# First head's queries and keys by a casting DMA, mask rows by DMA, and a fixed load order at the start of a fused attention and mixer kernel

## The chip, the cores and the metric

The kernel runs on one core of one Trainium2 chip. The metric is device time in microseconds: 287.15 us before the change, the median of 6 runs (286.35 to 287.81). A profile of one execution is used beside it. Engines in the profile: PE (TensorE matmul), PEld (TensorE weight load), DVE (VectorE), ACT (ScalarE), POOL (GpSimd) and SP (SyncE, here only a DMA queue). DMAs are also issued from ACT's and POOL's queues.

## The reference

A block-sparse attention is followed by a mixer. For each of 4 batches and 8 heads, 768 positions of 64 numbers:

```python
mask = np.abs(blk_i - blk_j) <= window            # blocks of 32, 24 of them
mask = mask | (blk_i == 0) | (blk_j == 0) | (blk_i == n_blocks - 1) | (blk_j == n_blocks - 1)
for qb in range(n_blocks):                        # and 3 sampled blocks for each
    for kb in sampled_blocks[qb]:
        mask[qb * block:(qb + 1) * block, kb * block:(kb + 1) * block] = True
scores = np.where(mask, scale * q @ k.T, -1e9)
attn = softmax(scores) @ v
...
# x is the attention's output, heads side by side: (4, 768, 512)
u = x + (x.transpose(0, 2, 1) @ U @ V).transpose(0, 2, 1)   # U 768x32, V 32x768
out = u + np.maximum(u @ w_ch1, 0) @ w_ch2                  # 512 -> 2048 -> 512
```

All inputs and the output are float32; the kernel computes in float16 with float32 sums.

## The kernel before

Work goes by pairs of heads, 16 pairs in all, four to a batch. Position p*6 + t of the sequence lies on partition p in slice t, so each head of q, k or v is loaded as 128 rows of 384 numbers. A pair's q and k are loaded in float32 by SP (`load_qk`, L147), cast to float16 by POOL (`cast`, L138) into a staging tile `stqld` or `stkld`, and turned on PE. Values are loaded and cast the same way (`load_v`, L160) into `vt`.

**Masking in the first batch (pairs 0 to 3).** The mask is put into the score's matmul. A head's query tile `qres[i]` has 64 rows of queries and 24 rows that say in one-hot form which block a position is in; the key tile `kres[i]` has 64 rows of keys and 24 rows of bias per block (0 or -240). Head 0 of a pair has its data in partitions 0 to 63 and mask rows from 64 on, head 1 the other way round (`drows`, `mrows`, L127). There are two such sets, used in turn by pairs; `second_set` (L310) fills the mask rows of the second from the first by DMA. The one-hot rows and the fixed part of the mask come from one constant in DRAM, `small_const`. The bias is worked out on DVE from the sampled block ids (`sb`) and that constant (L262 to L269), and PE spreads it over the positions (`mask_half`, L237).

A score (L652) is 128 keys by 768 queries in two matmuls; ACT makes its exponential (L661) into `est`; PE multiplies that with the values (L381). From pair 4 on, a mask tile is multiplied in on DVE instead (L690), made in the first batch from `kmask` (L611). The mixer's matmuls (L552 and L576) are woven in from then on.

**The order.** PE, DVE and ACT follow the program's order inside `manual_schedule` (L221 for the start, L782 for the rest; there SP too). In the rest, the order is written out as a string of words, `PLAN` (L403): `S` is a score, `e` its exponential, `A` a value product, `R` and `t` the turn of the next pair's q or k on PE and its copies on DVE (L624), `Z` and `z` the same for the first pair's second head (L295), `K` and `k` a part of the mask. It begins `S0 S3 e Z7 e z S0 S5 e Z2 e A7 z S3 A A e S0 S5 e A R2 e S3 t R1 e A A t S5 v e S3 S1`. POOL's instructions, and SP's at the start, are ordered by a planner, in general in the program's order. A DMA of SP or ACT takes one of eight semaphores in turn, and so waits for the DMA eight before it to land.

**The start before.** ACT issues the block ids, SP the constants, then q and k of head 0 and q and k of head 1 (L186), the values of pair 0, q, k and v of pair 1, the one-hot rows of head 1 (L311), and those of the second set. PE does nine warming matmuls (`keep_warm`, L229). DVE sets four tiles to zero (L226), casts head 0's q (L200), and ACT casts its k; PE turns both against the identity (`first_turn`, L204), and ACT and DVE copy the turned halves into `qres[0]` and `kres[0]` (`first_row`, L248). ACT copies head 0's one-hot rows (L255). `mask_row` (L245) copies the bias rows. POOL casts head 1's q and k, and PE turns them as words `Z` of the plan.

Of the kernel before, what the change touches and what calls it, by code (L numbers as in the profile page):

```python
# [21 lines left out]
def kernel(  # L22
# [80 lines left out]
    def psc2():  # L103
        ring["psc"] += 1
        return PS[:, (0, 3)[ring["psc"] % 2] :][:, 0:2]
# [8 lines left out]
    id16 = consts.tile([P, P], FP16)  # L114
# [21 lines left out]
    sts = {}  # L136
# [22 lines left out]

    def load_v(i):  # L160
        b, hp = divmod(i, HP)
        ld = ldpool.tile([P, 2, T, D], FP32, tag="ldv", name="vld")
        nc.sync.dma_start(
            out=ld,
            in_=v[b, 2 * hp : 2 * hp + 2].rearrange("h (p t) d -> p h t d", t=T),
        )
        cast(i, vts[b % 2][:, 2 * hp : 2 * hp + 2, :, 0:D], ld)
# [1 line left out]

    NPAIR = B * HP  # L170
    NPE = HP + 2
    nc.scalar.dma_start(
        out=sb[0:NB].rearrange("k z r w -> k (z r w)"),
        in_=sampled_blocks.bitcast(I32).rearrange("z r -> (z r)")[None, :].broadcast_to(
            [NB, NB * 6]
        ),
    )
    nc.sync.dma_start(out=small[0:NB, :], in_=small_dr.ap())
    nc.sync.dma_start(out=id16, in_=eye_dr.ap())
    lds = {}  # L180
    for h in range(2):
        for src, nm in ((q, "qld"), (k, "kld")):
            if h == 0:
                lds[nm] = ldpool.tile([P, 2, T, D], FP32, tag="ld" + nm, name=nm)
                sts[0, nm] = stpool.tile([P, T, 2, D], FP16, tag="st" + nm, name="st" + nm)
            nc.sync.dma_start(  # L186
                out=lds[nm][:, h], in_=src[0, h].rearrange("(p t) d -> p t d", t=T)
            )


    warm = nc.const_aps.tensor(1.0, [P, 512], mybir.dt.bfloat16)
    bias = consts.tile([P, 2, D], FP16)
    for vt in vts:
        nc.gpsimd.memset(vt[:, :, :, D : D + 1], 1.0)
    for tile_ in (Ut, Vt, kmask):
        nc.gpsimd.memset(tile_, 0.0)

    def first_cast(h, n, copy):
        nm = ("qld", "kld")[n]
        copy(out=sts[0, nm][:, :, h], in_=lds[nm][:, h])  # L200

    first_out = {}

    def first_turn(h, n, c):  # L204

        if n == 1:
            pt = psm([P, HS], FP32)
        elif c == 0:
            pt = pw[:, 1, 0:HS]
        else:  # L210
            pt = psc2()[:, 0, 0:HS]
        first_out[n, c] = pt
        for j in range(3):
            nc.tensor.matmul(
                pt[0:D, j * P : (j + 1) * P],
                sts[0, ("qld", "kld")[n]][:, 3 * c + j, h],
                id16,
                start=(j == 0), stop=(j == 2), skip_group_check=True,
            )

    with tc.manual_schedule(  # L221
        engines={mybir.EngineType.PE, mybir.EngineType.DVE, mybir.EngineType.Activation}
    ):
        nc.vector.memset(bias, 0.0)
        for res in (*qres, *kres):
            nc.vector.memset(res, 0.0)  # L226
        pw = psc2()

        def keep_warm(n, cols=512):  # L229
            for _ in range(n):  # L230
                nc.tensor.matmul(  # L231
                    pw[:, 0, 0:cols], warm[:, 0:P], warm[:, 0:cols], start=True, stop=True
                )

        pks = [bank(6, [P, HS], FP32), psm([P, HS], FP32)]

        def mask_half(c):  # L237
            nc.tensor.matmul(
                pks[c],
                bias[0:NB].rearrange("k a z -> k (a z)"),  # L240
                ohT[:, c * HS : (c + 1) * HS],
                start=True, stop=True,
            )

        def mask_row(h, c, copy):  # L245
            copy(out=kres[0][mrows[h], h, c * HS : (c + 1) * HS], in_=pks[c][mrows[h]])

        def first_row(n, c, copy):  # L248
            copy(
                out=(qres, kres)[n][0][drows[0], 0, c * HS : (c + 1) * HS],  # L250
                in_=first_out[n, c][0:D],
            )

        keep_warm(9)
        nc.scalar.copy(out=qres[0][mrows[0], 0, :], in_=ohT)  # L255
        first_cast(0, 0, nc.vector.tensor_copy)
        first_turn(0, 0, 0)
        first_turn(0, 0, 1)

        eq = consts.tile([P, NB, 3], FP32)  # L260
        a01 = consts.tile([P, NB], FP32)
        nc.vector.tensor_scalar(  # L262
            out=eq[0:NB], in0=sb[0:NB, :, :, 0], scalar1=iota, scalar2=-1.0,
            op0=ALU.is_equal, op1=ALU.add,
        )
        nc.vector.tensor_reduce(
            out=a01[0:NB], in_=eq[0:NB], axis=mybir.AxisListType.X, op=ALU.max
        )
        nc.vector.scalar_tensor_tensor(  # L269
            out=bias[0:NB, :, 0:NB], in0=a01[0:NB, None].broadcast_to([NB, 2, NB]),  # L270
            scalar=-MASK_BIAS, in1=ms[:, None].broadcast_to([NB, 2, NB]),
            op0=ALU.mult, op1=ALU.max,
        )
        first_cast(0, 1, nc.scalar.copy)
        first_turn(0, 1, 0)
        first_row(0, 0, nc.vector.tensor_copy)
        first_row(0, 1, nc.scalar.copy)
        mask_half(0)
        first_row(1, 0, nc.scalar.copy)
        first_turn(0, 1, 1)  # L280
        mask_half(1)
        keep_warm(2, 256)
        mask_row(0, 0, nc.vector.tensor_copy)
        first_row(1, 1, nc.vector.tensor_copy)
        mask_row(0, 1, nc.vector.tensor_copy)
        mask_row(1, 0, nc.vector.tensor_copy)
        mask_row(1, 1, nc.vector.tensor_copy)


    results = {}  # L290
# [4 lines left out]
    def last_turn(n, k_):  # L295
        pt = bank(k_, [P, S], FP16)
        for t in range(T):
            nc.tensor.transpose(
                out=pt[:, t * P : (t + 1) * P],
                in_=sts[0, ("qld", "kld")[n]][:, t].rearrange("p h d -> p (h d)"),  # L300
                identity=id16,
            )
        then(
            "z",
            lambda: nc.vector.tensor_copy(
                out=(qres, kres)[n][0][drows[1], 1, :], in_=pt[drows[1], :]
            ),
        )

    def second_set():  # L310
        nc.sync.dma_start(  # L311
            out=qres[0][mrows[1], 1, :], in_=small_dr.ap()[:, 2 * NB + 2 :]
        )
        for h in range(2):
            nc.sync.dma_start(
                out=qres[1][mrows[h], h, :], in_=small_dr.ap()[:, 2 * NB + 2 :]
            )
            nc.sync.dma_start(out=kres[1][mrows[h], h, :], in_=kres[0][mrows[h], h, :])
        nc.sync.dma_start(out=kmask[mrows[0], :], in_=kres[0][mrows[0], 0, :])

    def load_mix():
        uld = ldpool.tile([P, T, R], FP32, tag="ldu", name="uld", bufs=1)
        nc.sync.dma_start(out=uld, in_=moe_U.rearrange("(p t) r -> p t r", t=T))
        vld = ldpool.tile([P, 2, T, D], FP32, tag="ldv", name="vld")
        vld = vld.rearrange("p h t d -> p (h t d)")
        nc.sync.dma_start(out=vld[0:R, :], in_=moe_V)
        nc.gpsimd.tensor_copy(out=Ut[:, :, 0:R], in_=uld)
        nc.gpsimd.tensor_copy(
            out=Vt[0:R, :, :], in_=vld[0:R, :].rearrange("r (p t) -> r t p", t=T)
        )  # L330

    def load_w1(cs):
# [381 lines left out]

    bts[0] = Batch()
    pairs = {}
    for n in range(2):
        first_cast(1, n, nc.gpsimd.tensor_copy)
    load_v(0)
    load_qk(1)  # L720
    load_v(1)
    second_set()
    load_mix()

    def begin(i):
        if i and i % HP == 0:
            bts[i // HP] = Batch()
# [102 lines left out]
```

## Time and profile before

| what | value |
|---|---|
| median of 6 runs | 287.15 us |
| the profiled execution's own time | 287.17 us |
| its span | 285.4 us |
| PE busy in the span | 277.8 us |
| ACT busy | 179.6 us |
| DVE busy | 198.4 us |
| POOL busy | 69.5 us |

A line of the timeline gives start and length in us, engine, line of the kernel, operation, output <- input, shape and count; in brackets the idle time before it and what ended that. `SPq`, `ACTq` and `POOLq` are DMA issues. A busy PE is not PE at its peak: the ends of matmuls are modelled. The granted clock is 1.00 in every stretch.

### The profile page before, as it was taken

To read this page: it belongs to the slowest core of one execution; us is meant where nothing else is said; L and a number is where in the kernel's file an instruction comes from. 1 tells how busy PE (TensorE), PEld (TensorE's weight loads), DVE (VectorE), ACT (ScalarE), POOL (GpSimd) and SP (SyncE) were. 2 spreads that over 40 slices of the span, in tenths; PEclk is the share of its full clock that TensorE was granted. 3 is DMA by queue.
4 is the path that set the end of the run, shared out by engine and by line. 5 is a ranking of instruction groups with operands and counts; after the bars stand their busy time and mean duration, and the time that the engine had idled before them with its cause. 6 is when DMAs were issued, how large, how long until landed. Compare 5 with 4: busy or idle time off the path is not lost.

```text
span 285.4 us, 6732 instructions
## 1 busy us (share of the span) xinstructions
PE 277.8 (97%) x2771; PEld 163.9 (57%) x2771; DVE 198.4 (70%) x360; ACT 179.6 (63%) x212; POOL 69.5 (24%) x157
## 2 busy tenths in 40 slices
PE   8789999999999999999999999999999999999995
PEld 3557775657456654567556564565745565555553
DVE  7488989998768966788687885666866888231121
ACT  4799998885678566775776627777588730424200
POOL 4566133902242052500451032700310000000000
PEclk9999999999999999999999999999999999999999
DMA  5799979799271479108460398303741103001012
GB/s 155 243 283 289 226 207 214 150 143 226 58 230 39 91 227 253 58 24 222 100 214 2 95 234 203 135 20 59 225 87 39 39 37 87 17 0 40 37 55 92
DMA packets 46430, 36.78 MB, mean 129 GB/s; under 512 B 28000, under 2 KB 42912, under 8 KB 46400
## 3 DMA queue, kind: packets, MB, share of 16 engines
q1 hardware_dynamic: 43532, 32.02, 40.8%
q0 software_dynamic: 2688, 4.19, 8.3%
q8 instruction: 21, 0.34, 0.5%
q10 hardware_dynamic: 180, 0.15, 0.2%
q14 instruction: 9, 0.07, 0.1%
HBM read 27.66 MB, written 6.29 MB: 119 GB/s over the span
## 4 chain that ended last, share of the span: by engine, by line
PE 88%; DVE 8%; DMA 2%; issue 1%; ACT 0%; DVEq 0%
PE ps L552 29%; PE ps L576 28%; PE ps L381 11%; PE ps L675 9%; PE ps L652 3%; DMA qres<-small_const 2%; PE ps L465 2%; PE ps L499 2%; PE ps L231 1%; PE ps L596 1%; DVE xh L446 1%; DVE mask L619 1%; DVE xf L446 1%; PE ps L627 1%; DVE est L690 1%; DVE u L506 1%
## 5 line engine op out<-in xcount | busy, mean ns | idle before, releaser
L684 ACT ACTIVATE est<-ps 128x1536 f16<-128x1536 f32 x72 | 100.4, 1449 | 31.3 <-PE ps L675 31.3
L552 PE MATMUL ps<-uT,w1t 128*128 128x384 f16 x512 | 95.6, 326 | 0.4 <-DVE xf L509 0.2
L576 PE MATMUL ps<-w2t,tT 128*128 128x512 f16 x368 | 88.8, 379 | 0.0
L690 DVE TENSOR_TENSOR est<-est,mask 128x1536 f16<-128x1536 f16 x72 | 69.1, 962 | 13.4 <-ACT est L684 13.2
L564 ACT ACTIVATE tT<-ps 128x384 f16<-128x384 f32 x87 | 42.1, 493 | 54.0 <-PE ps L552 52.4
L552 PEld LDWEIGHTS <-w1t 128*128 128x128 f16 x512 | 47.4, 98 | 36.8 <-issue 6.6
L576 PEld LDWEIGHTS <-tT 128*128 128x128 f16 x368 | 34.4, 98 | 36.5 <-issue 2.9
L381 PEld LDWEIGHTS <-est 128*128 128x128 f16 x1152 | 40.8, 97 | 8.0 <-issue 2.3
L381 PE MATMUL ps<-vt,est 128*128 128x65 f16 x1152 | 43.2, 193 | 1.3 <-POOL vt L141 1.2
L566 DVE TENSOR_SCALAR tT<-ps 128x384 f16<-128x384 f32 x41 | 22.8, 555 | 30.6 <-PE ps L552 30.0
L144 POOL CAST stqld<-qld 128x192 f16<-128x192 f32 x40 | 15.4, 427 | 112.6 <-DMA qld<-in_q_dram 94.9
L661 ACT ACTIVATE est<-ps 128x768 f16<-128x768 f32 x48 | 35.2, 813 | 2.8 <-PE ps L652 2.8
L675 PE MATMUL ps<-qpl,kpl 64*128 64x512 f16 (+1 forms) x288 | 31.3, 325 | 0.0
L652 PE MATMUL ps<-qres,kres 128*128 128x384 f16 x96 | 22.4, 324 | 1.6 <-DVE kres L637 0.6
L584 DVE TENSOR_TENSOR of<-xf,ps 128x512 f32<-128x512 f32 x23 | 15.8, 685 | 9.8 <-PE ps L576 9.6
L675 PEld LDWEIGHTS <-kpl 64*128 64x128 f16 x288 | 11.7, 94 | 15.4 <-issue 9.5
L506 DVE TENSOR_TENSOR u<-xh,ps 128x384 f16<-128x384 f16 x28 | 15.4, 552 | 7.0 <-PE ps L499 6.1
L446 DVE TENSOR_TENSOR xh<-ps,rcp 128x384 f16<-128x384 f32 x32 | 17.8, 557 | 1.1
L446 DVE TENSOR_TENSOR xf<-ps,rcp 128x384 f32<-128x384 f32 x32 | 17.5, 547 | 0.0
L144 POOL CAST vt<-vld 128x192 f16<-128x192 f32 x40 | 15.3, 423 | 3.8 <-DMA vld<-in_v_dram 2.2
L144 POOL CAST stkld<-kld 128x192 f16<-128x192 f32 x40 | 16.0, 440 | 0.7 <-DMA kld<-in_k_dram 0.7
L509 DVE TENSOR_TENSOR xf<-xf,ps 128x384 f32<-128x384 f32 x28 | 15.4, 549 | 0.0
(78 smaller groups left out, 145.7 us busy)
## 6 DMA issues: line engine op xcount, KB each, us to landing
vld<-in_v_dram SPq DMA_DIRECT2D x16, 384.0 KB, 6.3
out_dram<-of SPq DMA_DIRECT2D x23, 256.0 KB, 4.0
qld<-in_q_dram SPq DMA_DIRECT2D x15, 384.0 KB, 4.4
kld<-in_k_dram SPq DMA_DIRECT2D x15, 384.0 KB, 4.7
w1t<-in_moe_w_ch_dram POOLq DMA_DIRECT2D x4, 512.0 KB, 10.5
w2t<-in_moe_w_ch_dram POOLq DMA_DIRECT2D x4, 512.0 KB, 7.4
qld<-in_q_dram SPq DMA_DIRECT2D x2, 192.0 KB
kld<-in_k_dram SPq DMA_DIRECT2D x2, 192.0 KB, 4.8
```

The source lines that it names most:

```text
L144: last = nc.gpsimd.tensor_copy(out=dst[:, h, ts], in_=ld[:, h, ts])
L381: nc.tensor.matmul(pav[:, sc, :], est[:, n, sc * P : (sc + 1) * P], vts[b % 2][:, 2 * hp + h, g, 0 : D + 1], start=(g == 0 and sc == 0), s ...
L446: self.last = nc.vector.tensor_tensor(out=dst, in0=pav[:, :, 0:D], in1=rcp[:, :, None].broadcast_to([P, T, D]), op=ALU.mult,)
L552: nc.tensor.matmul(pt, w1t[:, cc, jj * P : (jj + 1) * P], bts[b].uT[cc][:, c * HS : (c + 1) * HS], start=(cc == 0), stop=(cc == NCC - 1), ...
L564: nc.scalar.activation(out=dst, in_=pt, func=AF.Relu)
L566: nc.vector.tensor_scalar_max(out=dst, in0=pt, scalar1=0.0)
L576: nc.tensor.matmul(po, tts[b, c, jj][:, s * P : (s + 1) * P], w2t[:, jj, :], start=(jj == 0), stop=(jj == NJJ - 1),)
L652: nc.tensor.matmul(ps[:, c], kT[:, h, g * P : (g + 1) * P], qT[:, h, c * HS : (c + 1) * HS], start=True, stop=True,)
L661: lambda: nc.scalar.activation(out=dst, in_=ps, func=AF.Exp, scale=0.125),
L675: nc.tensor.matmul(units[h][:, u * S + lo : u * S + hi], kT[drows[h], g * P : (g + 1) * P], qT[drows[h], lo:hi], start=True, stop=True, sk ...
L684: nc.scalar.activation(out=both[h], in_=units[h].rearrange("p (g n) -> p g n", g=2), func=AF.Exp, scale=0.125,)
L690: lambda: nc.vector.tensor_mul(out=both[h], in0=both[h], in1=mask[:, 2 * j : 2 * j + 2, :]),
```

## The change

The first head's q and k are loaded by POOL's queue with a cast on the way, straight into float16 tiles `q0` and `k0`, from which `first_turn` reads. The one-hot rows of both heads of the first set come by DMA from SP (`one_hot`), after DVE has zeroed the query tile; ACT's copy of them is gone. The constant and the identity are issued by ACT, the block ids by SP. ACT begins with an exponential of one column. The head-0 half of the staging tile, which was the cast data, is set to zero by POOL, as the turn of head 1 still covers both halves. Zeroing moves: `kmask` from POOL to DVE, `qres[1]` and `kres[1]` from DVE to POOL. PE does seven warming matmuls, then the first half of the mask, then the turns; the copies are dealt out anew between ACT and DVE. SP's order at the start is now the program's, with `load_v(0)`, `load_qk(1)`, `load_v(1)`, `second_set` and `load_mix` moved into the first block, without change of their order among each other, save that `second_set` no longer has the first set's row and does a head's two DMAs in turn.

```diff
@@ -169,40 +169,58 @@
-    nc.scalar.dma_start(
-        out=sb[0:NB].rearrange("k z r w -> k (z r w)"),
...
-    nc.sync.dma_start(out=small[0:NB, :], in_=small_dr.ap())
-    nc.sync.dma_start(out=id16, in_=eye_dr.ap())
     lds = {}
-    for h in range(2):
-        for src, nm in ((q, "qld"), (k, "kld")):
-            if h == 0:
-                lds[nm] = ldpool.tile([P, 2, T, D], FP32, tag="ld" + nm, name=nm)
-                sts[0, nm] = stpool.tile([P, T, 2, D], FP16, tag="st" + nm, name="st" + nm)
-            nc.sync.dma_start(
-                out=lds[nm][:, h], in_=src[0, h].rearrange("(p t) d -> p t d", t=T)
-            )
-
+
+    firsts = []
+    for src, nm in ((q, "q0"), (k, "k0")):
+        firsts.append(consts.tile([P, T, D], FP16, name=nm))
+        nc.gpsimd.dma_start(
+            out=firsts[-1], in_=src[0, 0].rearrange("(p t) d -> p t d", t=T)
+        )
+
+    def first_load(n):
+
+        src, nm = ((q, "qld"), (k, "kld"))[n]
+        lds[nm] = ldpool.tile([P, 2, T, D], FP32, tag="ld" + nm, name=nm)
+        nc.sync.dma_start(
+            out=lds[nm][:, 1], in_=src[0, 1].rearrange("(p t) d -> p t d", t=T)
+        )
+        sts[0, nm] = stpool.tile([P, T, 2, D], FP16, tag="st" + nm, name="st" + nm)
+        nc.gpsimd.memset(sts[0, nm][:, :, 0], 0.0)
+        nc.gpsimd.tensor_copy(out=sts[0, nm][:, :, 1], in_=lds[nm][:, 1])
+
+    def one_hot(i, h):
+        nc.sync.dma_start(
+            out=qres[i][mrows[h], h, :], in_=small_dr.ap()[:, 2 * NB + 2 :]
+        )
...
-    for tile_ in (Ut, Vt, kmask):
-        nc.gpsimd.memset(tile_, 0.0)
-
-    def first_cast(h, n, copy):
-        nm = ("qld", "kld")[n]
-        copy(out=sts[0, nm][:, :, h], in_=lds[nm][:, h])
+    for tile_ in (qres[1], kres[1], Ut):
+        nc.gpsimd.memset(tile_.bitcast(FP32), 0.0)
+
+    def second_set():
+        for h in range(2):
+            one_hot(1, h)
+            nc.sync.dma_start(out=kres[1][mrows[h], h, :], in_=kres[0][mrows[h], h, :])
+        nc.sync.dma_start(out=kmask[mrows[0], :], in_=kres[0][mrows[0], 0, :])
...
             nc.tensor.matmul(
-                pt[0:D, j * P : (j + 1) * P],
-                sts[0, ("qld", "kld")[n]][:, 3 * c + j, h],
-                id16,
+                pt[0:D, j * P : (j + 1) * P], firsts[n][:, 3 * c + j, :], id16,
                 start=(j == 0), stop=(j == 2), skip_group_check=True,
             )
 
     with tc.manual_schedule(
-        engines={mybir.EngineType.PE, mybir.EngineType.DVE, mybir.EngineType.Activation}
+        engines={
+            mybir.EngineType.PE,
+            mybir.EngineType.DVE,
+            mybir.EngineType.Activation,
+            mybir.EngineType.SP,
+        }
     ):
+        nc.sync.dma_start(
+            out=sb[0:NB].rearrange("k z r w -> k (z r w)"),
...
+        nc.scalar.dma_start(out=small[0:NB, :], in_=small_dr.ap())
+        nc.scalar.dma_start(out=id16, in_=eye_dr.ap())
         nc.vector.memset(bias, 0.0)
-        for res in (*qres, *kres):
+        for res in (qres[0], kres[0], kmask):
             nc.vector.memset(res, 0.0)
+        for h in range(2):
+            one_hot(0, h)
+        for n in range(2):
+            first_load(n)
+        first = consts.tile([P, 1], FP32)
+        nc.scalar.activation(
+            out=first, in_=nc.const_aps.tensor(1.0, [P, 1], FP32), func=AF.Exp
+        )
...
-        keep_warm(9)
-        nc.scalar.copy(out=qres[0][mrows[0], 0, :], in_=ohT)
-        first_cast(0, 0, nc.vector.tensor_copy)
-        first_turn(0, 0, 0)
-        first_turn(0, 0, 1)
-
...
-        first_cast(0, 1, nc.scalar.copy)
-        first_turn(0, 1, 0)
-        first_row(0, 0, nc.vector.tensor_copy)
-        first_row(0, 1, nc.scalar.copy)
+        keep_warm(7)
         mask_half(0)
-        first_row(1, 0, nc.scalar.copy)
-        first_turn(0, 1, 1)
+        for c in range(2):
+            first_turn(0, c)
+            first_row(0, c, nc.scalar.copy)
+        first_turn(1, 0)
+        mask_row(0, 0, nc.vector.tensor_copy)
+        first_row(1, 0, nc.vector.tensor_copy)
+        first_turn(1, 1)
         mask_half(1)
         keep_warm(2, 256)
-        mask_row(0, 0, nc.vector.tensor_copy)
         first_row(1, 1, nc.vector.tensor_copy)
...
+        nc.gpsimd.memset(Vt, 0.0)
+        load_v(0)
+        load_qk(1)
+        load_v(1)
+        second_set()
+        load_mix()
...
-    for n in range(2):
-        first_cast(1, n, nc.gpsimd.tensor_copy)
-    load_v(0)
-    load_qk(1)
-    load_v(1)
-    second_set()
-    load_mix()
```

More of the change, by code (lines that the diff above doesn't have):

```diff
@@ L171 @@
     NPE = HP + 2
-    nc.scalar.dma_start(
-        out=sb[0:NB].rearrange("k z r w -> k (z r w)"),
-        in_=sampled_blocks.bitcast(I32).rearrange("z r -> (z r)")[None, :].broadcast_to(
-            [NB, NB * 6]
-        ),
-    )
-    nc.sync.dma_start(out=small[0:NB, :], in_=small_dr.ap())
-    nc.sync.dma_start(out=id16, in_=eye_dr.ap())
-    lds = {}
-    for h in range(2):
-        for src, nm in ((q, "qld"), (k, "kld")):
-            if h == 0:
-                lds[nm] = ldpool.tile([P, 2, T, D], FP32, tag="ld" + nm, name=nm)
-                sts[0, nm] = stpool.tile([P, T, 2, D], FP16, tag="st" + nm, name="st" + nm)
-            nc.sync.dma_start(
-                out=lds[nm][:, h], in_=src[0, h].rearrange("(p t) d -> p t d", t=T)
-            )
+    lds = {}
+    firsts = []
[17 more added lines that the diff above has]
+        )
     warm = nc.const_aps.tensor(1.0, [P, 512], mybir.dt.bfloat16)
@@ L194, with load_mix, first_turn @@
         nc.gpsimd.memset(vt[:, :, :, D : D + 1], 1.0)
-    for tile_ in (Ut, Vt, kmask):
-        nc.gpsimd.memset(tile_, 0.0)
-    def first_cast(h, n, copy):
-        nm = ("qld", "kld")[n]
-        copy(out=sts[0, nm][:, :, h], in_=lds[nm][:, h])
+    for tile_ in (qres[1], kres[1], Ut):
[5 more added lines that the diff above has]
+        nc.sync.dma_start(out=kmask[mrows[0], :], in_=kres[0][mrows[0], 0, :])
+    def load_mix():
+        uld = ldpool.tile([P, T, R], FP32, tag="ldu", name="uld", bufs=1)
+        nc.sync.dma_start(out=uld, in_=moe_U.rearrange("(p t) r -> p t r", t=T))
+        vld = ldpool.tile([P, 2, T, D], FP32, tag="ldv", name="vld")
+        vld = vld.rearrange("p h t d -> p (h t d)")
+        nc.sync.dma_start(out=vld[0:R, :], in_=moe_V)
+        nc.gpsimd.tensor_copy(out=Ut[:, :, 0:R], in_=uld)
+        nc.gpsimd.tensor_copy(
+            out=Vt[0:R, :, :], in_=vld[0:R, :].rearrange("r (p t) -> r t p", t=T)
+        )
     first_out = {}
-    def first_turn(h, n, c):
+    def first_turn(n, c):
         if n == 1:
@@ L221 @@
     with tc.manual_schedule(
-        engines={mybir.EngineType.PE, mybir.EngineType.DVE, mybir.EngineType.Activation}
-    ):
+        engines={
[4 more added lines that the diff above has]
+        }
+    ):
+        nc.sync.dma_start(
+            out=sb[0:NB].rearrange("k z r w -> k (z r w)"),
+            in_=sampled_blocks.bitcast(I32)
+            .rearrange("z r -> (z r)")[None, :]
+            .broadcast_to([NB, NB * 6]),
+        )
+        nc.scalar.dma_start(out=small[0:NB, :], in_=small_dr.ap())
+        nc.scalar.dma_start(out=id16, in_=eye_dr.ap())
         nc.vector.memset(bias, 0.0)
-        for res in (*qres, *kres):
+        for res in (qres[0], kres[0], kmask):
             nc.vector.memset(res, 0.0)
+        for h in range(2):
[5 more added lines that the diff above has]
+            out=first, in_=nc.const_aps.tensor(1.0, [P, 1], FP32), func=AF.Exp
+        )
         pw = psc2()
@@ L307, in last_turn @@
             ),
[L308 to L329, printed above, removed]
         )
```

## The prediction

> **What bounds the kernel now.** The page comes first: which engine fills the span, and where the chain that ended last begins.
>
> ```profile
> span 285.4 us, 6732 instructions
> PE 277.8 (97%) x2771; PEld 163.9 (57%) x2771; DVE 198.4 (70%) x360; ACT 179.6 (63%) x212; POOL 69.5 (24%) x157
> PE 88%; DVE 8%; DMA 2%; issue 1%; ACT 0%; DVEq 0%
> ```
>
> TensorE is the bound, so the change can only pay at the start, where PE still waits. The chain in order of time, first 20 us, says for what:
>
> ```profile
> 0.78 4.00 PE ps L231 x9
> ...
> 5.59 6.84 DMA qres<-small_const
> ...
> 12.57 0.49 PE ps L652 x2
> ```
>
> The one DMA in the chain is the one-hot rows of the second head (L311): issued at 5.59, landed at 12.43, because it queues behind all loads that SP issued before it. The timeline shows that and two other waits (last bracket: idle time before, and who ended it):
>
> ```profile
> 6.13 0.56 DVE L246 CAST kres<-ps 24x384 f16<-24x384 f32 x1 [0.31 <-PE ps L238]
> ...
> 6.83 0.81 PE L652 MATMUL ps<-qres,kres 128*128 128x384 f16 x4
> ...
> 9.77 0.83 POOL L141 CAST vt<-vld 128x768 f16<-128x768 f32 x1 [1.43 <-DMA vld<-in_v_dram]
> ...
> 10.65 0.34 PE L381 MATMUL ps<-vt,est 128*128 128x65 f16 x6 [1.21 <-POOL vt L141]
> ...
> 12.57 0.49 PE L652 MATMUL ps<-qres,kres 128*128 128x384 f16 x2 [0.56 <-DMA qres<-small_const]
> ...
> 13.07 0.50 PE L627 MATMUL ps<-id,stqld 128*128 128x128 f16 x6
> ...
> 15.92 0.48 PE L652 MATMUL ps<-qres,kres 128*128 128x384 f16 x2 [0.65 <-DVE kres L637]
> ```
>
> The first score starts at 6.83. PE then idles 1.21 us because the values land only at 9.72, and 0.56 us for the one-hot rows. The third wait (0.65) follows from the second: it is four DVE copies of 0.56 us behind the transposes of 13.07. Afterwards nothing is loose; busy time by stage (PE, PEld, DVE, ACT, POOL, clock, DMA share, GB/s):
>
> ```profile
> 7.00:17.40 10.40, 7.75 (x103) 5.39 (x102) 6.63 (x14) 8.36 (x11) 4.94 (x7) 1.00 0.74 233
> 17.40:44.50 27.10, 26.81 (x398) 19.90 (x395) 23.86 (x55) 26.82 (x37) 13.81 (x19) 1.00 0.97 247
> 44.50:100.00 55.50, 54.88 (x621) 32.66 (x620) 47.86 (x85) 40.48 (x40) 15.53 (x39) 1.00 0.68 145
> ```
>
> From 17.4 to 44.5 both ACT and PE are full, then PE. The written plan is unchanged, so whatever PE and ACT are ahead at 17.4 is what the end gains. The whole question is how much earlier that point comes.
>
> **The change part by part.** Times are in the profiled execution: span 285.40, own time 287.17, so 1.77 outside the span; the median of the runs shown is 287.15.
>
> 1. *First head's q and k by a casting DMA from POOL's queue.* Gone are DVE's cast (0.33), ACT's cast (0.51) and two SP issues (0.43 each). POOL pays two issues; the nearest rows are the four weight loads of the same queue, with as many rows (128):
>
> ```profile
> L334 POOL DMA_DIRECT2D w1t<-in_moe_w_ch_dram x4: 531/540/677, 19.8 to 24.8; - x4
> ```
>
> So q issues at 0.74 to 1.42 (the first took 677 ns), k to 1.96. From issue to first packet, the packet records show 1.16 us on SP's queue (q: 1.59 to 2.75), and on POOL's 1.64 and 1.45 for two w2 loads but 3.41 for the first w1 load (19.84 to 23.25). I take 1.55, since the 3.41 fell into a full DMA stretch (18 to 20: share 1.10) and the start is empty. First packet 2.3; q took 1.28 from there to landing and k 0.67 more: q at 3.6, k at 4.3 (before: 4.03 and 4.70, plus casts).
>
> [...] The 3.41 case gives k at 6.2.
>
> 2. *Order at the start.* ACT issues the mask constants and the identity, then loads its table (1.28, before at 2.49 after a DMA, now about 1.6): off the path. DVE has three memsets instead of four (0.70 + 0.11, twice, and half a one: until 3.0); then 0.24 + 0.21 + 0.20 give the bias at 3.75. Seven warming matmuls at 0.427 end at 3.77. PE's fixed order follows at the cold pace of the row before (107 ns per 128 columns): mask half 0.32, four turns 1.28, mask half 0.32, two fillers 0.43. First score at **6.1**, 0.7 earlier; DVE's key rows are done by 5.9. PE reaches the key turn at 4.73, so k at 4.3 hides. A later k means a first score 1.4 after its landing (two turns 0.64, mask half, fillers): 6.5 for 5.1, 7.6 for 6.2. Alone, this 0.7 is worth **nothing**: PE needs 2.6 us from first score to first value product (6.83 to 9.44) and waits for the values to 10.65. That cover also hides a k landing as late as about 6.6.
>
> 3. *When the values land.* SP's fixed order: block ids 0.74, two one-hot rows that wait for DVE's memset of the query tile (1.74) and need 0.40 each, second head's q and k (2.65, 3.1), values at about 3.6 (before 3.50). Queued behind that wait are all loads, hence the 0.1. The bytes ahead of the values are the same 4 x 192 KB; their first packet is at 2.3 instead of 2.75. Before, the sixteen completions of the values spread from 7.21 to 9.72, median 7.7: one slow DMA engine sets the landing. Bounds: 0.1 later (only the issue counts), or 1.9 earlier (no slow engine; PE's own path of 6.1 + 2.6 is then the limit). I take **0.5 earlier**, nearest to the 0.45 of the first packet. POOL is free: 1.96, marker columns 0.5, three memsets 0.74 + 0.74 + 0.4 (rows of Ut and Vt, 0.74 for 768 elements), two half-tile memsets and two casts 0.9 each pair, Vt 0.74: about 7.7. If POOL's memsets went by bytes, it would be 9.5, which would just begin to show.
>
> 4. *One-hot rows of the second head by DMA at the start.* They land near 4 instead of 12.43. PE then reaches the transposes of 13.07 at values + 1.70 (0.19 + 0.32 + 0.36 + 0.33 + 0.33 + 0.17) instead of + 2.42: **0.72** gained. DVE's four copies follow them and give it to the score of 15.92. ACT could follow by more (idle 0.22, 0.21 and 0.20 before its exponentials of 13.09, 14.95 and 17.46, and small ones), so PE's 0.72 counts. What is late next is the second pair's keys: POOL's cast ends 2.17 after that of the values, the turn comes at + 2.36: 0.2 spare.
>
> 5. *The rest.* SP's later order (second tile set, mix weights, pair 2) waits for mask rows at 7 to 8 and for a free DMA slot; each load is issued no later than now, and pair 2's queries (cast done 18.92, used 19.51) have 0.6 spare. If their landing didn't move, half the gain could be lost there. The extra memsets on POOL lie under its idle 2.96 us before 6.21.
>
> Sum: 0 + 0.5 + 0.72 = 1.22. 287.17 - 1.22 = **285.95**; the median before differs by 0.02, so I leave it.
>
> **The rivals.**
> - *The values come much earlier* (no straggling engine): 1.2 to 1.9 instead of 0.5, gain 1.9 to 2.6, **284.6 to 285.3**. For it: median 7.7; against: in the next three loads the slowest engine was also about a microsecond behind.
> - *The gain stays at the loads*: the values land 0.1 to 0.6 later, as SP issues them later and the casting loads share the same sixteen engines (DMA 0.76 to 1.06 busy from 5 to 11), or pair 2's queries take the gain back. Gain 0.1 to 0.6: **286.6 to 287.1**, no measurable change. The 1.21 us wait speaks for it: PE's start is not what counts.
> - *Slower: POOL's queue starts late and is starved.* The 3.41 us row repeats, q and k share the engines with q, k and v of SP's queue, and land near 8.5. First score then at 8.5 + 1.4 = 9.9, first value product at 12.5, 1.85 late, less 0.72: about 1.1 lost, **288.3**; worse up to 290. It decides from k at 7.4 on (first score 8.8, product 11.4, even). The w1 row speaks for it; against it, at the start SP's first big packet comes at 3.85, behind POOL's.
> - *The change doesn't do what it says*: not likely; every wait named is on a DMA that it moves.
>
> **How the numbers follow.** Forecast (285.3 to 286.4) 0.54; values much earlier 0.16; gain stays at the loads 0.20; slower 0.10. A measurement of this kernel tells about 0.2% (0.57 us) from no change: faster 0.70, same 0.20, slower 0.10. The range 284.8 to 287.4 leaves out a part of the second case and of the last two.
>
> **What would show it.** Right: first score near 6.1; PE's wait for the values still there, ending near 10.1; no wait on the one-hot rows; the transposes of 13.07 near 11.9; score of 15.92 near 14.7; ACT's last 128x768 exponential 1.2 earlier than 44.42. Wrong: k landing after 6.6; values after 10.3; a new PE wait on POOL's casts (second head, second pair); or the lead at 17.4 lost by 44.5.

## The result, and the profile after

The changed kernel takes **288.95 us** (median of 28 runs, 287.91 to 289.76) against 287.48 for the kernel before, measured beside it (65 runs). The ratio of after to before is 1.0044, 95% interval 1.0034 to 1.0054: it is slower, by about 1.5 us (0.44%). The forecast was 285.95, faster, with a range to 287.4. The profiled execution took 289.47 us, its span 287.5.

The page of the changed kernel, the same three rows as before:

```profile
span 287.5 us, 6723 instructions
...
PE 279.2 (97%) x2769; PEld 165.1 (57%) x2769; DVE 200.3 (70%) x358; ACT 178.4 (62%) x211; POOL 72.9 (25%) x162
...
PE 87%; DVE 8%; DMA 2%; SPq 1%; issue 1%; DVEq 0%
```

TensorE still fills 97% of the span. The span grew by 2.1 and PE's busy time by 1.4, with two matmuls fewer: part of the loss is matmuls that ran slower, not matmuls that waited. The chain in order of time says where to look (start, length, what):

```profile
2.87 3.26 DVE eq L293
...
6.16 0.23 DVE a L297
...
6.41 0.21 DVE bias L300
...
6.66 0.50 PE ps L275
7.16 1.42 PE ps L232 x12
...
9.55 1.28 PE ps L669 x4
```

In the chain of before, PE's warming matmuls stood in its place (0.78 to 4.78). Now one instruction of VectorE, the comparison of the sampled block ids with the row numbers (`eq`, L293), holds 3.26 us of it. The timeline has the same moment on three engines, then the points that the prediction named:

```profile
1.24 0.68 POOL L177 DMA_DIRECT2D q<-in_q_dram  x1 [0.79 <-POOLq L823]
1.91 0.55 POOL L177 DMA_DIRECT2D k<-in_k_dram  x1
2.44 0.55 POOL L200 MEMSET vt<- 128x48 f16 x2
2.59 1.05 POOL L202 MEMSET qres<- 128x768 f32 x1
2.87 3.25 DVE L293 TENSOR_SCALAR eq<-sb,small 24x72 f32<-24x72 int32 x1
3.55 0.76 POOL L202 MEMSET kres<- 128x768 f32 x1
4.23 0.44 POOL L202 MEMSET Ut<- 128x384 f32 x1
4.59 0.44 POOL L189 MEMSET stqld<- 128x384 f16 x1
4.95 0.44 POOL L189 MEMSET stkld<- 128x384 f16 x1
5.31 0.76 POOL L321 MEMSET Vt<- 128x768 f16 x1
...
6.66 0.50 PE L275 MATMUL ps<-small,bias 24*128 24x384 f16 x1 [2.74 <-DVE bias L300]
8.72 0.83 POOL L141 CAST vt<-vld 128x768 f16<-128x768 f32 x1 [0.96 <-DMA vld<-in_v_dram]
9.34 1.48 PE L669 MATMUL ps<-qres,kres 128*128 128x384 f16 x4
...
13.18 0.46 PE L398 MATMUL ps<-vt,est 128*128 128x65 f16 x6
14.99 0.50 PE L644 MATMUL ps<-id,stqld 128*128 128x128 f16 x6
17.91 0.48 PE L669 MATMUL ps<-qres,kres 128*128 128x384 f16 x2 [0.46 <-DVE kres L654]
```

In the kernel before, the same instruction took 0.24 us, and a cast of VectorE just ahead of it 0.33. POOL was idle then: the last bracket says that it had been so for 2.96 us when it began its own cast at 6.21.

```profile
4.08 0.33 DVE L200 CAST stqld<-qld 128x384 f16<-128x384 f32 x1
4.33 0.24 DVE L262 TENSOR_SCALAR eq<-sb,small 24x72 f32<-24x72 int32 x1
...
6.21 0.50 POOL L200 CAST stqld<-qld 128x384 f16<-128x384 f32 x1 [2.96 <-DMA qld<-in_q_dram]
```

In the changed kernel, the instruction handles the same 72 numbers on 24 partitions. Its two inputs had landed by then (the block ids at 2.62, the constant at 2.44), so it did not wait for data. It ends at 6.12. From 2.44 to 6.07 POOL zeroes tiles without a break: each memset starts before the one ahead of it has ended. The comparison begins 0.43 after the first of them and ends 0.05 after the last.

PE waits 2.74 us for the bias. The first score starts at 9.34 instead of 6.83, and four half scores take 1.48 where they took 0.81: PE is at half pace. The trace's clock records put full pace at 13.41, against 5.66 before. (The granted clock stands at 1.00 in both stretches; the durations show this, that column doesn't.) The one-hot rows no longer make anyone wait, and the values' cast at 8.72 is long done when PE asks for it at 13.18. So the waits that the change aimed at are gone, and the score that started at 15.92 starts at 17.91.

From there on the delay is only handed on: the window (busy PE, PEld, DVE, ACT, POOL, clock, DMA share, GB/s) shows the next stage about as full as before (ACT 28.62 of 29.10, against 26.82 of 27.10), and the last group of ACT's 128x768 exponentials ends at 46.41 instead of 44.42.

```profile
17.40:46.50 29.10, 28.37 (x416) 20.99 (x415) 25.80 (x59) 28.62 (x40) 13.31 (x19) 1.00 0.89 230
```

### The profile page after: what moved, and what is told of

Same layout as the page of the kernel before. It is cut to its first block, busy times and chain, and to the rows that moved or that the text cites. A ratio compares the mean times of both kernels' runs of the same rounds, so it can differ in the third digit from the quotient of the medians.

```text
span 287.5 us, 6723 instructions
## 1 busy us (share of the span) xinstructions
PE 279.2 (97%) x2769; PEld 165.1 (57%) x2769; DVE 200.3 (70%) x358; ACT 178.4 (62%) x211; POOL 72.9 (25%) x162
## 4 chain that ended last, share of the span: by engine, by line
PE 87%; DVE 8%; DMA 2%; SPq 1%; issue 1%; DVEq 0%
PE ps L569 28%; PE ps L593 28%; PE ps L398 11%; PE ps L692 9%; PE ps L669 3%; PE ps L482 2%; DMA vld<-in_v_dram 2%; PE ps L516 2%; PE ps L613 1%; DVE eq L293 1%; DVE xh L463 1%; DVE mask L636 1%; DVE xf L463 1%; DVE u L523 1%; DVE est L707 1%
## 5 line engine op out<-in xcount | busy, mean ns | idle before, releaser
L669 PE MATMUL ps<-qres,kres 128*128 128x384 f16 x96 | 23.8, 341 | 0.8 <-DVE kres L654 0.5
L144 POOL CAST stkld<-kld 128x192 f16<-128x192 f32 x40 | 16.6, 457 | 1.6 <-DMA kld<-in_k_dram 1.5
## 6 DMA issues: line engine op xcount, KB each, us to landing
w1t<-in_moe_w_ch_dram POOLq DMA_DIRECT2D x4, 512.0 KB, 10.1
```

Of the source, the lines that this page charges most:

```text
L144: last = nc.gpsimd.tensor_copy(out=dst[:, h, ts], in_=ld[:, h, ts])
L669: nc.tensor.matmul(ps[:, c], kT[:, h, g * P : (g + 1) * P], qT[:, h, c * HS : (c + 1) * HS], start=True, stop=True,)
```

## The experiments

The theory: POOL's unbroken memsets hold up VectorE's comparison, which reads and writes SBUF (the on-chip memory in which the tiles lie), for as long as they run; the comparison holds up the bias; the pause makes PE start its work at half pace. Rivals: the loss lies in the casting DMAs or in the loads' new order; or the late comparison is only a symptom of late data. Ratios are to the kernel before, which was measured beside each run (medians of 287.27 to 287.48, so a difference of 0.2 us between two rows says nothing). "Comparison" is the length of that instruction; the last three columns are starting times in the profiled execution.

| run | edit | us | ratio (95%) | comparison | first score | first value product | score of 15.92 |
|---|---|---|---|---|---|---|---|
| before | | 287.48 | 1 | 0.24 | 6.83 | 10.65 | 15.92 |
| after | | 288.95 | 1.0044 (1.0034 to 1.0054) | 3.25 | 9.34 | 13.18 | 17.91 |
| e1_eq_psum | after, comparison's output in PSUM | 285.71 | 0.9944 (0.9932 to 0.9957) | 0.20 | 6.45 | 10.05 | 14.66 |
| e2_pool_waits | after, POOL's memsets behind the comparison | 286.03 | 0.9956 (0.9944 to 0.9969) | 0.18 | 6.71 | 10.30 | 14.97 |
| e6_half_run | after, half of the memsets behind it | 286.82 | 0.9982 (0.9967 to 0.9997) | 1.86 | 6.87 | 10.52 | 15.13 |
| e3_warm16 | after, 16 warming matmuls | 287.38 | 1.0020 (1.0005 to 1.0035) | 3.25 | 8.44 | 11.12 | 15.75 |
| e5_before_memsets | before, four memsets of one tile more | 287.32 | 0.9998 (0.9982 to 1.0014) | 0.80 | – | – | – |
| e5b_before_unbroken | before, five memsets of five tiles more | 289.15 | 1.0058 (1.0035 to 1.0081) | 0.48 (cast 2.75) | 9.71 | 13.24 | 17.79 |
| e4_before_onehot | before, one-hot rows issued early | 285.39 | 0.9934 (0.9922 to 0.9946) | 0.24 | 7.19 | 9.76 | 14.32 |
| e8_before_v_first | before, values loaded first | 287.24 | 0.9996 (0.9983 to 1.0008) | 0.24 | 7.04 | 9.75 | 15.96 |
| e7_late_onehot | e1, one-hot rows late again | 287.05 | 0.9988 (0.9976 to 1.0000) | 0.21 | 6.62 | 9.30 | 14.89 |
| e9_before_onehot_act | e4 from ACT's queue | 286.21 | 0.9958 (0.9944 to 0.9972) | 0.24 | 6.69 | 9.51 | 14.06 |
| e10_psum_onehot_act | e1, one-hot rows from ACT's queue | 288.34 | 1.0018 (1.0001 to 1.0036) | 0.20 | 9.74 | 12.52 | 17.14 |

One check on the whole table: the profiled execution's own time less the start of its last column is 271.25 for before (287.17 - 15.92), 271.56 for after (289.47 - 17.91), and between 271.25 and 271.62 in every run with that column but e9, which has a wait behind it. So what each kernel wins or loses is decided before 18 us.

**Take the comparison's output out of SBUF (e1).** The output goes to a bank of PSUM (the memory that receives TensorE's results) instead of SBUF; every memset stays where it is.

```diff
-        eq = consts.tile([P, NB, 3], FP32)
+        eq = bank(1, [P, NB, 3], FP32)
```

> The changed kernel, with one edit: the result of VectorE's first mask instruction (block ids compared with the row's number, 0.24 us before the change and 3.25 us after it) goes to PSUM instead of SBUF. The data it waits for, its engine and its place are the same. Theory 1 ([...]): [...]the instruction takes about 0.25 us, the first mask half on TensorE comes at 3.8 instead of 6.66, the first score near 6.1, the first value product near 9.6, and the time is about 285.7, 0.6% below the kernel before the change. Rival (the instruction waits for late data, the block ids or the constant, or is slow for another reason): it still ends near 6.1 and the time stays at 289.

285.71 us. The timeline of e1:

```profile
2.87 0.20 DVE L293 TENSOR_SCALAR ps<-sb,small 24x72 f32<-24x72 int32 x1
...
3.85 0.49 PE L275 MATMUL ps<-small,bias 24*128 24x384 f16 x1
...
6.45 0.81 PE L669 MATMUL ps<-qres,kres 128*128 128x384 f16 x4
...
10.05 0.34 PE L398 MATMUL ps<-vt,est 128*128 128x65 f16 x6 [1.04 <-POOL vt L141]
```

The comparison starts at the same 2.87 from the same data and takes 0.20: the rival of late data falls. The bias is in PE at 3.85, the first score is at 6.45 at full pace, and the wait for the values is back. This one line of the code is the difference between 288.95 and 285.71 us: 3.24 by the medians, 2.9 by the ratios.

**Take the memsets away in time (e2, e6).** In e2, POOL first copies a result of VectorE (`gate`), and all its memsets follow; in e6 only the staging tiles' and `Vt`'s do. The core of e2:

```diff
...
+        opened = nc.gpsimd.tensor_copy(out=gate[0:NB], in_=a01[0:NB])
+        with tc.issue_after(opened.ins):
+            for tile_ in (qres[1], kres[1], Ut):
+                nc.gpsimd.memset(tile_.bitcast(FP32), 0.0)
...
```

> The changed kernel, with GpSimd's memsets put behind the mask instruction: GpSimd first copies the result of VectorE's reduction (24x24), and only then zeroes the second tile set, the mixer tiles and the staging halves. The mask instruction is as in the changed kernel. Theory 1: it takes 0.25 to 0.4 us (the two small memsets of the value tiles end at 3.0), the first score comes near 6.1, time about 285.8, with GpSimd's casts of the second head some 1 us later, under cover. Rival (late data): the instruction still ends at 6.1 and the time stays at 289. If the first kernel of this job gains and this one doesn't, it is not the memsets.

286.03 us. In e2:

```profile
2.87 0.18 DVE L289 TENSOR_SCALAR eq<-sb,small 24x72 f32<-24x72 int32 x1
```

The output is in SBUF as in the change, so it is POOL's work that held the comparison, and PSUM is not needed for the cure. What the memsets hold, no trace shows; shown is that the comparison is free without them (0.18) and, beside them, with its output in PSUM (0.20 in e1). e6 leaves the memsets up to `Ut` where they are:

> The changed kernel with GpSimd's run of memsets cut in two: the second tile set and the mixer's U stay ahead, then GpSimd waits for VectorE's mask reduction, and the staging halves and V come behind. [...]the mask comparison ends with the first part, at about 4.7 instead of 6.1 (2.87 plus 1.9 us), the bias is there at 5.3, and the time lies between the changed kernel and the one whose memsets all wait: 286.5 to 288. If one memset alone could hold it up, the comparison would end at 3.7 (the end of the memset that runs when it starts); if it waits for data, at 6.1.

```profile
2.87 1.86 DVE L291 TENSOR_SCALAR eq<-sb,small 24x72 f32<-24x72 int32 x1
...
4.24 0.44 POOL L200 MEMSET Ut<- 128x384 f32 x1
```

It ends at 4.73, 0.05 behind the end of `Ut`'s memset; in the change it ends 0.05 behind that of `Vt`'s. The comparison's length follows the length of POOL's run: 0.18 without one, 1.86 with half, 3.25 with all. e6 takes 286.82 us, 0.8 more than e2, with runs from 285.62 to 288.03.

**The clock's part (e3).** Sixteen warming matmuls in place of seven bridge the pause; the comparison stays late.

```diff
-        keep_warm(7)
+        keep_warm(16)
```

> The changed kernel with 16 instead of 7 warming matmuls, which fill the 2.7 us in which TensorE waits for the mask bias. The mask instruction stays slow. Theory 2 (a good part of the loss is the cold clock: TensorE's pause puts off the full clock from 5.7 to 13.4 us): the full clock comes near 6 us, the first mask half stays at 6.7, the first score comes near 8.2 instead of 9.3, the first value product near 10.8 instead of 13.2, time about 286.9, 2 us below the changed kernel. Rival (the lateness of the bias alone makes the loss, the clock does not matter): time stays within 0.3 us of 289.

287.38 us, where 286.9 was expected. In e3:

```profile
0.78 5.10 PE L268 MATMUL ps<-const-bfloat16-1.0 128*128 128x512 bf16 x16 [0.78 <-PEq L823]
6.84 0.33 PE L275 MATMUL ps<-small,bias 24*128 24x384 f16 x1 [0.96 <-DVE bias L300]
8.44 0.82 PE L669 MATMUL ps<-qres,kres 128*128 128x384 f16 x4
```

The bias is as late as in the change, but the mask half takes 0.33 instead of 0.50 and the four half scores 0.82 instead of 1.48 (full pace from 3.77). So e1 wins back two things, PE's half pace (from the change to e3) and the delay itself (from e3 to e1). By the medians they are 1.57 (288.95 - 287.38) and 1.67 us (287.38 - 285.71); by the ratios 0.7 and 2.2; by the profiled executions (289.47, 287.29, 286.28) 2.2 and 1.0. The runs of e3 spread from 287.01 to 289.63. That both parts count is shown; how the loss divides between them is not.

**Put the cause into the kernel before (e5, e5b).** First, more memsets of a tile that it already zeroes:

```diff
-    for tile_ in (Ut, Vt, kmask):
+    for tile_ in (Ut, Vt, kmask, Vt, Vt, Vt, Vt):
```

> The kernel before the change with the suspected cause alone: GpSimd zeroes one of its mixer tiles four more times (0.74 us each), so that its memsets run without a break to about 6.2 us instead of 3.25. Nothing else is touched. Theory 1 (a run of GpSimd memsets keeps VectorE from instructions[...]): VectorE's cast of the first queries (4.08, 0.33 us) and the mask comparison (4.33, 0.24 us) do not end before about 6.2, the first queries' turn on TensorE comes after 6.3 instead of at 4.70, the first score near 8.5 to 9, and the time is 0.7 to 2 us above the kernel before. Rival (the changed kernel's slow comparison came from its DMA order or its GpSimd DMAs): both stay at 0.3 us and the time stays the same.

287.32 us: nothing lost, and the expectation missed. In its trace PE's warming matmuls took 11.93 us instead of 4.00, so nothing of PE is read from it, only VectorE's and POOL's first 7 us:

```profile
3.19 3.22 POOL L196 MEMSET Vt<- 128x768 f16 x4
...
4.11 0.82 DVE L200 CAST stqld<-qld 128x384 f16<-128x384 f32 x1
4.85 0.80 DVE L262 TENSOR_SCALAR eq<-sb,small 24x72 f32<-24x72 int32 x1
```

Four memsets of one tile take 3.22 us, 0.81 each, where a memset of this shape takes 0.74: each waits for the one ahead of it, and between them is a pause of some 0.06. They end at 3.92, 4.72, 5.61 and 6.40. The cast ends at 4.93 and the comparison at 5.65, 0.21 and 0.05 behind such an end: VectorE gets in at the pauses. The bias comes at 6.13 instead of 5.05; that no time is lost fits the wait of the kernel before for the one-hot rows, under which it can hide. What an unbroken run costs, the next one shows. Five memsets of five different tiles don't wait for each other:

```diff
-    for tile_ in (Ut, Vt, kmask):
+    for tile_ in (Ut, Vt, kmask, *(mask[:, g] for g in range(5))):
```

> The kernel before with five more GpSimd memsets, each of another tile (parts of the mask tile, which is written for good only later), so that no wait stands between them and the run goes on to about 6.7 us. In the earlier kernel of this kind four memsets of one tile had pauses of 0.06 us between them, and VectorE's instructions got in. Theory 1: now the cast of the first queries and the mask comparison both end only after 6.7, the first score comes near 9.4, the score that waits for the one-hot rows is reached at 13.7 to 14.5 instead of 12.57, and the time is 1.2 to 2.3 us above the kernel before. Rival (a GpSimd memset holds VectorE up only for its own length, pauses or not): the two end at 5.7 and the time stays the same.

289.15 us. In e5b:

```profile
3.19 3.43 POOL L196 MEMSET mask<- 128x768 f16 x5
4.08 2.75 DVE L200 CAST stqld<-qld 128x384 f16<-128x384 f32 x1
6.75 0.48 DVE L262 TENSOR_SCALAR eq<-sb,small 24x72 f32<-24x72 int32 x1
```

Five in 3.43, 0.67 apart at 0.74 each, so that each starts before the one ahead has ended. It is the cast now that meets the run: 2.75 us instead of 0.33, to 6.83, 0.21 behind the run's end at 6.62. PE waits 2.11, full pace comes at 12.89, and the kernel before is now as slow as the changed one (1.0058 and 1.0044, with overlapping intervals). The cause is shown alone, with none of the change in the kernel.

**What the rest of the change is worth (e4, e8, e7).** One part of it alone, in the kernel before: the one-hot rows of the second head issued just after VectorE's memsets.

```diff
+        nc.sync.dma_start(
+            out=qres[0][mrows[1], 1, :], in_=small_dr.ap()[:, 2 * NB + 2 :]
+        )
...
-        nc.sync.dma_start(
-            out=qres[0][mrows[1], 1, :], in_=small_dr.ap()[:, 2 * NB + 2 :]
-        )
```

> The kernel before the change, with one part of the change alone: the one-hot rows of the first pair's second head are loaded by a DMA that SP issues ahead of the first pair's values instead of behind the second pair's loads. By the prediction's step 4 the wait of 0.56 us at 12.57 goes, the transposes of 13.07 come 0.72 us earlier, and the time is 0.7 us (0.25%) below the kernel before. Rival (the values, one issue later, land later by as much, or another wait takes its place): 0 to 0.3 us.

285.39 us, the lowest of all kernels run: one moved DMA beats both kernels. In e4:

```profile
7.19 0.81 PE L652 MATMUL ps<-qres,kres 128*128 128x384 f16 x4
...
9.76 0.35 PE L381 MATMUL ps<-vt,est 128*128 128x65 f16 x6
...
11.46 0.50 PE L627 MATMUL ps<-id,stqld 128*128 128x128 f16 x6
```

The expected 0.7 is there: from the first value product to the transposes it is 1.70 (11.46 - 9.76) where it was 2.42. The gain is more than double because the values came earlier too: issued 0.44 later than before, they landed at 8.35 instead of 9.72, and the product starts 0.89 earlier. The moved DMA need not be the reason: in e5b, which issues these loads at the same times as the kernel before, they landed at 8.28. So the landing moves by more than a microsecond between executions, and the 9.72 of before's trace, on which the prediction's 1.21 us wait rests, need not be its usual value. Of the 1.60 between the two traces at the last column, 0.89 is the values' and 0.71 the one-hot rows'. Are early values enough without the rows? e8 brings only the values forward:

```diff
+        if h == 1:
+            load_v(0)
         for src, nm in ((q, "qld"), (k, "kld")):
...
-    load_v(0)
```

> The kernel before, with the first pair's values loaded ahead of the second head's queries and keys. By the prediction's step 3 (values that land earlier pay one to one) the wait of 1.21 us shrinks and the time falls by up to 1 us. If the one-hot rows at 12.43 set the time whatever the values do, TensorE only waits longer there, and the time stays within 0.3 us of the kernel before.

287.24 us, no change. In e8:

```profile
9.75 0.34 PE L383 MATMUL ps<-vt,est 128*128 128x65 f16 x6
...
12.61 0.48 PE L654 MATMUL ps<-qres,kres 128*128 128x384 f16 x2 [1.50 <-DMA qres<-small_const]
```

The product starts 0.90 earlier, and the wait for the one-hot rows grows from 0.56 to 1.50: it takes back all of it. e7 asks the same of the changed kernel, e1 with the second head's one-hot rows behind the pair's loads again:

```diff
-        for h in range(2):
-            one_hot(0, h)
+        one_hot(0, 0)
...
         load_v(1)
+        one_hot(0, 1)
```

> The kernel whose mask comparison goes to PSUM (285.71), with the one-hot rows of the first pair's second head put back behind the second pair's loads on SP's queue, as in the kernel before. If that late DMA was what held the kernel before, and everything else in the change is off the path, the rows land near 12.3, TensorE waits for them, and the time goes back to 287.0 to 287.5. By the prediction's step 4 alone (0.72) it goes to 286.4. If the rest of the change carries the gain, it stays at 285.7.

287.05 us against 285.71. In e7:

```profile
9.30 0.36 PE L398 MATMUL ps<-vt,est 128*128 128x65 f16 x6
...
11.47 0.48 PE L669 MATMUL ps<-qres,kres 128*128 128x384 f16 x2 [0.80 <-DMA qres<-small_const]
```

PE waits 0.80 for the rows. The two profiled executions differ by only 0.20 us (286.48 and 286.28), the medians by 1.34; e1's profiled execution is the slowest of its six, with values that landed at 9.11. So the trace of e7 shows the wait, and its usual size only the medians (the rows landed at 11.34 here, at 12.43 in before).

Behind the cure, then, the change is worth what the one moved DMA is worth: 285.71 in e1, 285.39 in e4, with overlapping intervals. The casting DMAs and the fixed order add nothing that was measured.

**Two tries for more (e9, e10).** e9 issues e4's rows from ACT's queue, to keep SP's loads free:

```diff
-        nc.sync.dma_start(
+        nc.scalar.dma_start(
             out=qres[0][mrows[1], 1, :], in_=small_dr.ap()[:, 2 * NB + 2 :]
```

> The kernel before with the one-hot rows of the second head loaded early, as in the one that reached 285.39, but issued from ScalarE's queue instead of SP's, so that SP's loads keep their times. The values are issued at 3.5 instead of 3.94. TensorE no longer waits for them in either, so by the new theory only an earlier first score counts: near 6.9 instead of 7.19, time 285.0 to 285.4. If the landing of the values still limits, it gains up to 0.4 more.

286.21 us, a miss. The start is the earliest of all (14.06 in the last column), then:

```profile
15.19 0.34 PE L613 MATMUL ps<-qres,kmask 128*128 128x384 f16 x1 [0.64 <-DMA kmask<-kres]
```

The planner, which orders SP's loads there, had put the mixer's second load and both loads of key rows ahead of the mask's rows (`kmask`), which were issued at 11.62 instead of 9.07 in e4; 0.64 was given back at 15.19.

e10 does the same in e1, for both heads' rows:

```diff
-        nc.sync.dma_start(
+        (nc.scalar, nc.sync)[i].dma_start(
             out=qres[i][mrows[h], h, :], in_=small_dr.ap()[:, 2 * NB + 2 :]
```

> The changed kernel with the mask comparison in PSUM, and both one-hot rows of the first set issued from ScalarE's queue, so that SP issues the second head and the values about 1.2 us earlier. The values then land near 7.9 instead of 8.3 to 9.1; the first head's casting DMA has more company and lands up to 0.5 later. First score 6.4 to 6.8, first value product near 9.2 without a wait, time 284.9 to 285.5. If the casting DMA is pushed behind SP's loads, the first score comes after 7.2 and it is no better than 285.7.

288.34 us, the largest miss. In e10:

```profile
1.25 0.37 SPq L185 DMA_DIRECT2D qld<-in_q_dram  x1
...
1.92 0.55 POOL L177 DMA_DIRECT2D k<-in_k_dram  x1
...
8.12 0.85 PE L232 MATMUL ps<-id,k 128*64 128x128 f16 x6 [3.03 <-DMA k<-in_k_dram]
```

SP no longer waits for VectorE's memset, so its loads leave 1.26 us earlier, from 1.25 on instead of 2.51. The first head's keys, issued by POOL at 1.92 as in the change, land at 8.08 instead of 4.83 (5.21 in e1), and PE waits 3.03 for them. What keeps them back, these runs don't tell. Nor does it strike every time, by the run times: of e10's 22 runs 14 took 288.21 to 289.26 us, and 8 took 285.88 to 287.34, in part below the kernel before. The profiled one is of the 14.

## Why the prediction was wrong

**Step 2 failed**, at "then 0.24 + 0.21 + 0.20 give the bias at 3.75". The 0.24 came from a row in which POOL was idle (it idled until 6.21 while VectorE compared); the step used it at a place where the change had put eight memsets of POOL beside it, which step 3 of the prediction lists itself. The comparison took 3.25, the bias came at 6.61. The price of an instruction was carried over without the work that ran beside it.

**No step asks what GpSimd's memsets cost VectorE.** The other direction, VectorE's memsets beside a DMA of GpSimd's queue, cost nothing that the trace shows: the first packet of q left at 2.62, 1.38 after its issue, no later than the 1.45 and 1.64 of the w2 loads, while VectorE's memsets ran until 2.96. What decided this case is that VectorE is held up, and not by one memset (the longest here took 1.05) but by the whole unbroken series: the comparison took 3.25 in the change; it ended at a pause in e5 (0.80 long) and at the series' end in e6 (at 4.73).

**Step 5 priced POOL's extra memsets at nothing** because they "lie under its idle 2.96 us before 6.21". POOL was idle there, as said; the cover was checked for POOL's own time, not for VectorE's work beside it, where the comparison took 3.25 instead of 0.24.

**The half pace was in step 2, but as a constant.** It counted cold matmuls up to 6.1 and full pace behind; with the pause, half pace lasted to 13.41. The arithmetic of the first value product closes with this: the first score 3.24 late (9.34 - 6.1), the way from it to the product 1.24 longer (3.84 instead of 2.6), less the 1.40 that the values' wait had covered (10.1 - 8.7), gives 3.08: 13.18 against the 10.1 of the forecast.

**What held.** With the comparison freed (e1), the steps come out: first score 6.45 (6.1), the end of PE's wait for the values 10.05 (10.1), the transposes 11.74 (11.9), the score behind the copies 14.66 (14.7), 285.71 us (285.95). Between the two traces, steps 3 and 4 add up as written: 0.60 from the values (10.65 to 10.05, 0.5 foreseen) and 0.73 from the rows (2.42 to 1.69, 0.72 foreseen). The 0.60 is in part luck, as the values' landing moves by more than that between executions (e5b). What the sum hides is that the two are not equal: early values without the rows are worth little (e8, e7), while the moved rows, priced at 0.72, brought 1.9 us alone (e4), as the values landed early there without further help. In step 1, q landed at 4.38 and k at 4.83 instead of 3.6 and 4.3: POOL's first issue was at 1.24, not at 0.74, and 1.38 passed to the first packet (1.55 taken). Step 2 had cover for this in "a k landing as late as about 6.6", and e1 shows it (k at 5.21, first score 6.45, values still awaited).

**The rivals.** "Slower: POOL's queue starts late and is starved" gave 288.3, near the measured time by luck, since its mechanism wasn't at work: its threshold was k at 7.4, and k landed at 4.83. e10 shows that it exists: k at 8.08 and 288.34 us. What kept it away in the change is, by e10, a wait that step 3 counted as a delay of 0.1, SP's for VectorE's memset of the query tile: SP's loads left from 2.51 on there, from 1.25 on in e10. "The gain stays at the loads" and "the values come much earlier" were not decided in the change, since the values landed at 8.66 and nobody waited for them.

## What to carry to other kernels

A duration from a profile holds for the company that the instruction had: before moving memsets or casts to GpSimd, list what VectorE does in the same microseconds, and price a comparison or cast from SBUF to SBUF among it at the end of GpSimd's unbroken series, not at its own row (here 3.25 us for a comparison of 0.24, 2.75 for a cast of 0.33). If one of them gates TensorE, send its output to PSUM (0.20 in e1), order GpSimd's work behind it (0.18 in e2), or leave gaps (0.80 in e5). And try the one moved DMA that the chain of waits names before a rearrangement around it: here it was worth 1.9 us alone, and the rest nothing that was measured.

## What the hardware showed beyond the prediction

- GpSimd's memsets only write, and VectorE's comparison handles 72 numbers on 24 partitions; still it took 3.25 us, and a cast of VectorE 2.75 (e5b). The comparison ended 0.05 us behind a memset's end in the change, e6 and e5, the cast 0.21 behind one in e5 and e5b. Pauses of some 0.06 us between memsets were enough to let VectorE in (e5). It also got in at the last memset's end when POOL's next instruction, a cast, had begun 0.03 (the change) or 0.06 us (e5b) before; why a cast behind a memset differs there from a memset is open.
- POOL's casts held VectorE too: in e5b the comparison took 0.48 and ended 0.05 behind a cast of POOL (7.19), and the bias instruction took 0.38 (e3) and 0.34 (e5b) instead of 0.20, ending 0.05 behind one (6.73, 7.81).
- VectorE's memset of `kmask`'s 384 words ran from 2.58 to 2.96, beside POOL's first memsets, and kept its pace (0.38, where 768 words take 0.70): this instruction was not held.
- PE's full pace after a pause: with PE busy from its first matmul on, it came between 3.0 (e3) and 5.9 us (e4) after it; behind a pause of 2.74 us, 6.75 us after the restart (6.66 to 13.41), and 6.0 us in e5b behind one of 2.11 (6.89 to 12.89). In e2, gaps of 0.36 and 0.76 us were followed by half pace from 6.98 to 10.39 (four half scores in 1.24 and 1.49 us, where 0.81 is the full pace). What sets the moment of full pace within these ranges is not shown.
- A casting DMA of POOL's queue landed 3.3 us later (8.08 against 4.83) when SP's loads were issued ahead of it (the profiled execution of e10).
